# Zeros moved behind a softmax, a band matrix copied in four pieces, and a new order of instructions

## The chip, the cores and the metric

The kernel runs on one core of one Trainium2 chip. The metric is the device time of one execution in microseconds (us). Before the change three runs gave 176.5, 177.24 and 177.67; the median is 177.24. A profile of one further execution was taken, which itself took 177.53.

Engines are named as the profile names them: PE multiplies matrices (PEld is its loading of the stationary operand), DVE and ACT work on vectors, POOL and SP issue DMAs here.

## The reference

Two stages follow each other on x (8 batches, 4224 tokens, 192 channels, float32). The first is a causal convolution over 7 tokens, with one set of 7 weights for each of 8 heads (24 channels each), the weights being a softmax. The second mixes tokens through a 64 wide product, without a softmax:

```python
w = np.exp(weight - weight.max(-1, keepdims=True)); w = w / (w.sum(-1, keepdims=True) + 1e-9)   # (8, 7)
y = np.einsum('hk,bskhg->bshg', w, x_unf).reshape(B, S, D)      # x_unf: the 7 tokens up to s, zeros ahead of the first
W_tok = (1 / np.sqrt(64)) * np.einsum('bsd,btd->bst', y @ w_q, y @ w_k)
out = np.maximum(np.einsum('bst,btd->bsd', W_tok, y), 0) @ w_out
```

Since nothing non-linear stands between W_tok and y, the token by token matrix is never formed: W_tok y is (y w_q) (w_k^T y^T y), and y^T y is a 192 x 192 Gram matrix.

## The kernel before

**Tiling.** Tokens of a batch are cut into 35 chunks of 122 (NCC, CW); a chunk is loaded as 128 rows, 6 of them from the chunk ahead, and cast to bf16 on its way into XW. Groups of chunks share a load: four groups of 9 (the last of 8) in the first batch, two of 18 and 17 in the others. POOL issues all loads of x; SP issues the small weights and the stores.

**Steps of one batch**, with the kind that each has in the code and PE's matmuls in it:

- conv: for two heads, BAND (128 x 128 for each head, a banded matrix of the 7 softmax weights) times the group's columns, four matmuls; ACT or DVE copies the result from PSUM into Y (line 671).
- tr_lo, tr_hi: transposes of Y, channels 0 to 127 (16 matmuls for 8 chunks) and 128 to 191 (10 or 11), copied by DVE into YTL (698) and YTH (733).
- wq: y w_q from the transposes (lines 751 and 755), copied into WQT (771).
- gram: six chunks of Y times themselves, 18 matmuls (787), added up in a PSUM bank of their own.
- g, turn, gt, m, ms: the Gram matrix is copied, turned and multiplied with w_k, which gives the mixing weights MSB and MBD of the batch.
- mix_lo, mix_hi: WQT with the mixing weights (878, 890); ACT or DVE applies the relu on its way to RT (907, 908).
- fin_hi, fin_lo: RT times w_out (935 and the helper at 391, 392); the result is copied into one of four output buffers (970), and SP stores it (978).

PE works in one of two tilings of its array, 128x64 for most steps and 64x128 for mix_lo and fin_hi (COL2 and ROW2 in the code). Lines 391, 392 and 395, 396 are helpers that issue two half wide matmuls or transposes; conv, fin_lo, tr_lo and m all pass through them.

**What sets the order.** Each step is an Op with its engine, an assumed length, what it needs, and a due time vt, which is overwritten by the next number of the list TURNS. The Planner lays the Ops out engine by engine: among the Ops that can start it takes the one with the smallest vt, where a step of PE in the other tiling counts STAY more. Each engine then runs its own list in that order, with semaphores for what an Op needs from another engine; what is listed as `after` orders the plan without a wait of its own. Nothing is decided at run time. `op.lands` tells the Planner when a load of x is assumed to have arrived.

**The beginning.** DVE sets zeros and ones in many small buffers (lines 409 to 422), POOL makes an identity, DVE and PE make helper matrices from it. When the 56 convolution weights have landed, DVE computes their softmax (461 to 492) with ACT's exponential, and `taps` (494) spreads it. From it PE fills two PSUM banks, with eight matmuls each, that hold the bands; ACT copies one half and DVE the other into BAND (527). The first conv needs both.

Of the kernel before, what the change touches and what calls it, by code (L numbers as in the profile page):

```python
# [10 lines left out]


TURNS = [
    int(t) / 1000
    for t in """
-9360 -9860 -8870 -8880 -9260 -9760 -9760 -9160 -9060 -8960 -8910 -8910 -8860 -9360 -9310 -9360 -9360
-9300 -9290 -9280 -8360 -8260 -8210 -8360 -8160 -7960 -7910 -7860 -7360 -7260 -6960 -7260 -4360 -10360
-4260 -4160 -4060 -4040 -3360 -3260 -3160 -4360 -4360 -4360 -4360 -4360 -4360 -4360 -4360 -4360 -4360
-3360 -3340 -3260 -3240 -2360 -2340 -2260 -2240 -1360 -1340 -1260 -1240 -360 -340 -260 -240 640 660 740
760 1640 1660 1740 1760 2640 2660 2740 2760 -480 -5256 -3269 -5639 -2436 -6119 -4785 -6922 -2697 -6547  # L20
-2900 -8184 -3709 -11773 -2741 -3270 -6090 -11945 -3405 -6849 535 -5290 -3070 -5355 -2914 -5199 -4248
-3270 -5203 -8176 -5200 -3617 1049 7270 -1527 1452 -125 437 -1115 2575 669 4462 -4008 2241 -736 2188
-3392 2688 -366 4671 2314 4774 1510 -5859 -1080 1650 3655 -2805 -2225 2863 3712 -4982 -214 3624 -440
5811 168 -43 -4182 2328 1099 2977 4333 5544 2125 -4960 -5487 -5264 -3044 -1246 -5292 -632 -6217 -764
-74 -1078 1645 -1059 -604 310 -1847 1633 809 1261 1148 1774 613 1995 -221 2133 3240 -1868 3227 -220 725
-412 3895 1345 -3908 -437 2412 1145 -3912 1759 7529 -2401 -2511 -376 -45 -770 179 75 1157 1606 377 1178
2478 1419 2696 -2691 660 4785 4565 7183 -1945 323 1366 4118 -874 -955 202 -527 -342 -901 930 -907 356
2535 1985 1382 772 4127 1260 -1111 124 1160 1068 -949 2843 737 1947 1165 1141 1963 1865 1015 1391 1447
1702 -74 1049 2157 -573 -696 2171 3091 -3875 1621 1815 2057 1336 1560 3406 350 3930 1811 1631 806 1533
-2176 120 -160 307 697 392 -607 2158 1443 1095 4683 784 2578 2771 4703 2742 7357 3260 5899 3463 6217  # L30
3645 8560 -333 6048 2165 -3227 -299 4804 1442 -269 2464 1033 2330 -2282 2380 4417 716 -49 3007 5023
2635 1331 4441 4948 2995 6849 3538 5333 2785 2768 -3179 -2909 4430 6167 8185 2441 2170 3478 2909 2541
554 -2341 2444 1927 -821 1930 2471 1683 3865 3015 2812 1681 1913 2901 2236 -1040 2160 2775 2437 2022
2264 1982 2456 530 2945 -625 83 2391 2437 -247 4869 10274 3843 686 -2295 3278 468 -2877 2621 3234 3552
5619 5142 2314 3447 -712 2811 2566 3158 2537 2842 2785 -1373 2551 2194 3151 4852 2972 5013 3067 6779
3044 1235 3763 8267 3776 5123 4769 7025 4778 6514 4876 4862 2843 3189 4464 -186 3400 3287 1517 170 3082
4632 173 2822 4141 2345 4919 -1156 3870 4328 3579 2730 2456 3119 1411 4084 5177 4842 -327 4148 4784
2483 12403 11388 12726 1688 187 6372 10131 3246 4258 -1702 3458 4182 -118 2930 2729 1882 4669 8253 3861
3544 1615 3872 -172 2986 3160 3716 -1740 4531 9062 4005 3598 4951 3990 4363 2435 3391 -188 774 5121
6256 1049 3585 3961 4077 3890 4171 3621 2923 4666 7097 2748 2343 3820 2734 3811 2033 5780 3818 8021  # L40
2648 2954 4015 5571 3280 -1286 3326 1296 4205 -77 4486 1455 4875 3311 5075 4171 5445 4695 5467 3840
5547 6065 4545 4764 3889 874 4988 5384 3296 1407 5065 3706 4229 1167 4799 5495 -1008 2735 5015 4824
-216 1086 4797 3220 6247 4075 6903 8096 2585 2446 2397 3366 12419 11466 9645 4504 4002 2353 3004 4592
2447 1923 4855 3304 3544 3930 4268 4563 -31 1642 3776 4290 -862 3100 4826 6478 4160 4860 2445 3040 6705
3413 4148 6792 4180 4104 2785 4391 4686 4414 786 5937 2381 5714 4010 4678 4791 3602 4621 5486 -3702
4694 4691 4776 4745 8565 4811 2733 1579 4439 3726 3846 1552 3006 3416 5091 3731 3114 391 4950 -191 4947
1241 5561 6938 5922 7844 6076 5816 6857 5549 6431 8495 5919 4361 1180 965 5336 3713 5074 2853 2377 5685
3499 1703 6336 5580 6743 3976 5914 890 3735 -850 6119 5447 4947 4119 5702 6592 2952 2914 3851 5062
11027 10134 10283 4336 4832 2354 5585 5204 5235 5902 4279 5332 6811 4930 5452 70 7184 7777 5311 5310
3592 2752 3699 4914 5160 5093 886 6992 7265 5826 4610 2412 5386 6402 2677 5391 5863 3510 6078 4797 3048  # L50
3549 7308 4286 5112 2810 5621 5940 3872 3652 3847 6176 6516 2312 5811 4551 3444 5310 2800 3910 6703
2902 3118 6150 4601 5838 5604 6069 7926 5802 5058 6795 5408 6694 6497 7055 7466 7544 6117 8040 8562
2857 4878 6430 1709 6339 6247 4084 2149 3587 4651 7375 5911 5923 8233 4224 5104 7135 8548 7626 1422
6752 7520 5954 8811 9981 10001 3331 2861 1100 5523 5736 7942 8989 6855 6991 3418 3771 5267 6754 6792
5257 8583 2774 5930 5621 6098 8589 5981 7588 10163 5667 7262 8790 2009 6160 6573 7890 9275 9286 4367
8366 1994 4430 8376 2928 6391 6798 7671 9079 8471 6945 8447 929 3104 8245 1738 6621 7113 7765 8298
10610 7609 8976 2499 6811 5339 3124 4383 3701 4861 7650 5674 5118 6955 3022 7026 1967 7057 1554 7391
6867 7378 5794 8478 7540 10493 11198 10567 7886 9868 8667 7608 6132 7813 12143 8053 10500 4734 5726
10278 10809 6108 7660 6892 9279 8811 10480 9400 11789 6610 6051 11636 12987 12320 10573 10429 10064
11172 6766 7180 6653 8881 8940 8302 8163 3734 5115 8337 5917 10881 1732 6196 10991 548 6570 3947 6628  # L60
5684 11786 5374 8456 5972 5205 7358 2365 6800 7531 8553 12143 9541 7507 4239 2615 6653 8229 3661 7031
8556 8852 7269 9218 4711 5758 2449 5650 7927 7690 7261 10545 9140 8476 10487 4525 3241 2208 7451 8457
7788 6544 11624 6678 6638 3216 7890 3616 6282 3822 7930 5698 8782 6900 4062 5129 6641 6131 8120 8832
8094 4423 8160 8786 8210 8027 5877 5536 6062 1738 8351 8563 8713 4799 8391 5602 10941 9278 9705 9844
6685 7724 8581 9175 4769 3738 8621 7276 9572 10940 8347 11120 8993 5619 8811
""".split()
]

# [35 lines left out]
class Planner:  # L104
# [3 lines left out]
    LAT = {"PE": 240.0, "ACT": 145.0, "DVE": 140.0, "POOL": 150.0, "SP": 0.0}  # L108
    SWITCH = 145.0

    STAY = 0.865

    HOLD = 1

    def __init__(self, nbank, first_bank):
        self.ops = []
# [163 lines left out]
def bass_lightweight_conv__then__hypermixer_token_mlp_kernel(  # L280
# [9 lines left out]
    H, KC = weight.shape  # L290
# [15 lines left out]
    t = 0  # L306
# [37 lines left out]
    BAND = sbuf("band", [128, H, 128], BF16)  # L344
# [29 lines left out]
    def bank(i, n=1):  # L374
        return PS[:, i * 512 : (i + n) * 512]

    def add(*a, dma=None, kind=None, **k):
        op = Op(*a, **k)
        op.dma = dma
        op.kind = kind  # L380
        op.vt = TURNS[len(planner.ops)]
        return planner.add(op)
# [11 lines left out]
    def turn_halves(e, out, in_, identity):  # L394
# [11 lines left out]
        vt=-9,  # L406
# [3 lines left out]
    zero_w = add("DVE", lambda e, op: e.memset(WQT[64:128, :, wq_cols[-2] :], 0.0), 150, vt=-8.51)  # L410
# [15 lines left out]
        lambda e, op: e.affine_select(  # L426
            IDENT[:, :], IDENT[:, :], [[-1, 128]], ALU.is_equal, 0.0, base=0, channel_multiplier=1
        ),
        1250,
        needs=[one],  # L430
        vt=-9,
    )
# [22 lines left out]
    own = add(  # L455
        "DVE",
        lambda e, op: e.tensor_reduce(OWN[:, :], IDENT[:, :].rearrange("p (k i) -> p i k", i=16), AX.X, ALU.add),
        200, needs=[ident], vt=-8.92)


    mx = add("DVE", lambda e, op: e.tensor_reduce(WMX[:, :], WT_F[:, :, :], AX.X, ALU.max), 150, needs=[load_w], vt=-8)
# [39 lines left out]
    )  # L501
    taps.needs.append(own)


    bands = []
    for q0, engine in ((0, "ACT"), (4, "DVE")):

        def spread(e, op, q0=q0):
            last = None
            for q in range(q0, q0 + 4):  # L510
                last = halves(
                    e,
                    bank(op.bank)[:, (q - q0) * 128 : (q - q0 + 1) * 128],
                    STEPT[0:112, 112 - 16 * q : 240 - 16 * q],
                    TAPS[0:112, :, :].rearrange("p i h -> p (i h)"),
                    start=q == q0,
                    stop=q == q0 + 3,
                    skip_group_check=True,
                )
            return last  # L520

        fill = add("PE", spread, 260, needs=[taps, stept], banks=1, vt=-7 + 0.1 * q0)

        def band(e, op, q0=q0, fill=fill):
            dst = BAND[:, :, 16 * q0 : 16 * q0 + 64]
            src = bank(fill.bank).rearrange("p (j h) -> p h j", h=H)
            return e.copy(dst, src) if op.engine == "ACT" else e.tensor_copy(dst, src)  # L527

        bands.append(add(engine, band, 550, drains=fill, vt=-6.9))


    load = {}
    at = [5000.0]

    def gen_load(b, gi):
        sem = semaphore(f"s_x{b}_{gi}")
# [19 lines left out]
                )  # L556
            )

        at[0] += len(cs) * 260.0
        load[b, gi] = []  # L560
        for k, part in enumerate(parts):
            first = (b, gi) == (0, 0) and part[0].shape[1] > 1 and len(part[0].shape) == 3
# [7 lines left out]
                vt=-10 if first else -4 + b + gi * 0.1 + 0.02 * k,  # L570
            )
            op.tail = 1500.0
            op.lands = at[0]
            load[b, gi].append(op)

    for gi in range(len(groups_of(0))):
# [482 lines left out]
```

## Time and profile before

| | us |
|---|---|
| median of three runs (lowest, highest) | 177.24 (176.5, 177.67) |
| the profiled execution | 177.53 |
| its span, first to last instruction | 175.7 |
| first convolution on PE | 8.76 |
| first record of the granted clock at full speed | 15.10 |
| last load of x landed | 106.0 |
| last matmul ended | 170.84 |
| last store landed | 175.13 |

The span is 1.8 us shorter than the execution's own time, since it counts from the first instruction to the last. All times in views are from the beginning of the span. A line of the timeline gives start, length, engine, line of the kernel, operation, what it writes and reads, and how often in a row; idle time of the engine before it and what ended that stand in brackets. [...]

In the list of loads, x of the first batch lands at 6.77, 10.79, 13.13 and 15.14 in its four groups, and of the second at 21.30 and 25.59.

### The profile page before, as it was taken

Reading aid. Unit: us, or ns where it says so; the run is one execution under the profiler, and the core shown is the slowest. Engines: PE = TensorE matmul, PEld = TensorE weight load, DVE = VectorE, ACT = ScalarE, POOL = GpSimd, SP = SyncE. Lnnn points to the kernel's source line nnn. Section 1 sums busy time; section 2 is a strip of 40 time slices with the busy share of each in tenths; the row PEclk is TensorE's granted clock in tenths of the full one; section 3 lists DMA queues with packets and bytes.
Section 4 is the critical chain, followed back from the end, with each engine's and each line's share of the span. In section 5 each row is a group of like instructions: output and inputs, shape, how many; then the busy total and the mean of one; then the engine's idle time right before and its main releaser. Section 6 shows DMA issues by size and latency. Waiting matters only on the chain.

```text
span 175.7 us, 7099 instructions
## 1 busy us (share of the span) xinstructions
PE 157.1 (89%) x3226; PEld 121.7 (69%) x3226; DVE 118.0 (67%) x216; ACT 123.5 (70%) x206; POOL 30.3 (17%) x39
## 2 busy tenths in 40 slices
PE   0289799888999999899989979999999999999990
PEld 0179666776787787668778766878767777877550
DVE  6556587765766677586787738689688675765740
ACT  3243677597787948668648747888888896698980
POOL 7999452524230000000000000000000000000000
PEclk9999999999999999999999999999999999999995
DMA  3999999999999999999999999067283045987787
GB/s 30 162 189 186 205 191 193 191 196 277 193 279 194 286 309 268 343 250 243 304 264 282 237 194 348 24 244 297 103 343 127 4 175 216 356 347 309 265 303 262
DMA packets 48157, 40.36 MB, mean 230 GB/s; under 512 B 37632, under 2 KB 40960, under 8 KB 48128
## 3 DMA queue, kind: packets, MB, share of 16 engines
q0 software_dynamic: 36128, 13.61, 65.1%
q1 hardware_dynamic: 12000, 26.31, 40.9%
q8 instruction: 25, 0.41, 0.9%
q14 instruction: 4, 0.03, 0.1%
HBM read 27.56 MB, written 25.95 MB: 305 GB/s over the span
## 4 chain that ended last, share of the span: by engine, by line
PE 88%; issue 4%; DVE 3%; ACT 2%
PE ps L391 25%; PE ps L787 14%; PE ps L935 8%; PE ps L392 7%; PE ps L395 6%; PE ps L726 6%; PE ps L878 5%; PE ps L751 4%; PE ps L890 4%; PE ps L755 4%; PE ps L396 3%; ACT rt L907 1%; ACT out_sb L970 1%; DVE band L527 0%; DVE xw L416 0%
## 5 line engine op out<-in xcount | busy, mean ns | idle before, releaser
L970 ACT COPY out_sb<-ps 128x768 f32<-128x768 f32 (+1 forms) x46 | 34.7, 768 | 15.1 <-PE ps L392 11.3
L671 ACT CAST y<-ps 122x816 bf16<-122x816 f32 (+3 forms) x46 | 35.7, 791 | 13.2 <-PE ps L392 12.8
L907 ACT ACTIVATE rt<-ps 128x1024 bf16<-128x1024 f32 (+3 forms) x44 | 34.1, 800 | 6.4 <-PE ps L878 4.5
L787 PE MATMUL ps<-y 122*64 122x192 bf16 (+4 forms) x840 | 33.8, 222 | 2.2 <-issue 2.2
L970 DVE COPY out_sb<-ps 128x768 f32<-128x768 f32 (+1 forms) x26 | 21.6, 840 | 19.7 <-PE ps L392 18.5
L392 PE MATMUL ps<-wol,rt 128*64 128x192 bf16 x264 | 33.9, 255 | 1.0 <-issue 1.0
L787 PEld LDWEIGHTS ps<-y 122*64 122x64 bf16 (+1 forms) x840 | 31.1, 112 | 4.9 <-issue 2.8
L565 POOL DMA_DIRECT2D xw<-in_x_dram x34 | 29.9, 893 | 22.3 <-issue 21.5
L391 PE MATMUL ps<-wol,rt 128*64 128x192 bf16 x264 | 33.7, 255 | 0.0
L391 PE MATMUL ps<-xw,band 128*64 128x432 bf16 (+3 forms) x144 | 31.8, 335 | 1.5 <-DVE band L527 0.9
L392 PE MATMUL ps<-xw,band 128*64 128x432 bf16 (+3 forms) x144 | 32.1, 337 | 1.1 <-issue 1.1
L391 PEld LDWEIGHTS ps<-wol,rt 128*64 128x64 bf16 x264 | 24.1, 138 | 8.1 <-issue 2.0
L908 DVE TENSOR_SCALAR rt<-ps 128x512 bf16<-128x512 f32 (+3 forms) x36 | 23.6, 674 | 8.2 <-PE ps L878 7.6
L671 DVE CAST y<-ps 122x864 bf16<-122x864 f32 (+3 forms) x26 | 23.6, 912 | 8.0 <-PE ps L392 7.5
L698 DVE COPY ytl<-ps 128x976 bf16<-128x976 bf16 (+1 forms) x40 | 23.0, 591 | 3.9 <-PE ps L396 3.3
L392 PEld LDWEIGHTS ps<-wol,rt 128*64 128x64 bf16 x264 | 24.1, 138 | 1.2 <-issue 1.2
L396 PE MATMUL ps<-ident,y 122*64 122x122 bf16 x280 | 21.1, 219 | 0.0
L395 PE MATMUL ps<-ident,y 122*64 122x122 bf16 x280 | 21.0, 219 | 0.0
L935 PE MATMUL ps<-woh,rt 64*128 64x192 bf16 x264 | 20.4, 250 | 0.2 <-ACT rt L907 0.2
L395 PEld LDWEIGHTS ps<-ident,y 122*64 122x64 bf16 x280 | 18.1, 112 | 2.0 <-issue 0.5
L726 PE MATMUL ps<-ident,y 122*64 122x122 bf16 (+1 forms) x344 | 17.1, 220 | 1.3 <-DVE y L671 0.7
L396 PEld LDWEIGHTS ps<-ident,y 122*64 122x64 bf16 x280 | 17.7, 112 | 0.0
(95 smaller groups left out, 218.8 us busy)
## 6 DMA issues: line engine op xcount, KB each, us to landing
out_dram<-out_sb SPq DMA_DIRECT2D x28, 768.0 KB, 5.1
xw<-in_x_dram POOLq DMA_DIRECT2D x7, 816.0 KB, 33.2
xw<-in_x_dram POOLq DMA_DIRECT2D x7, 768.0 KB, 33.7
out_dram<-out_sb SPq DMA_DIRECT2D x8, 384.0 KB, 3.3
xw<-in_x_dram POOLq DMA_DIRECT2D x2, 432.0 KB, 8.3
out_dram<-out_sb SPq DMA_DIRECT2D x8, 96.0 KB, 4.3
xw<-in_x_dram POOLq DMA_DIRECT2D x1, 384.0 KB, 5.2
xw<-in_x_dram POOLq DMA_DIRECT2D x8, 45.8 KB, 25.0
```

The lines of the kernel that those rows point to most:

```text
L391: e.matmul(out[0:64], lhsT[:, 0:64], rhs, **k)
L392: return e.matmul(out[64:128], lhsT[:, 64:128], rhs, **k)
L395: e.transpose(out[0:64], in_[:, 0:64], identity)
L396: return e.transpose(out[64:128], in_[:, 64:128], identity)
L565: lambda e, op, part=part: e.dma_start(*part),
L671: return e.copy(dst, src) if op.engine == "ACT" else e.tensor_copy(dst, src)
L726: last = e.transpose(ps[64 * i : 64 * i + HI, o : o + w], Y[0:w, yb, c, LO:D], IDENT[0:w, 0:w])
L787: mm = e.matmul(bank(GB)[p : p + 64, o : o + z - r], Y[0:w, yb, c, r : r + 64], Y[0:w, yb, c, r:z], start=st, stop=end, skip_group_check=True,
L907: return e.activation(dst, src(), AF.Relu)
L908: return e.tensor_scalar(dst, src(), 0.0, None, op0=ALU.max)
L935: last = e.matmul(bank(op.bank + a)[:, o : o + D], RT[64 * a : 64 * a + HI, slot, 2, i:n:nt], WOH[64 * a : 64 * a + HI, :], start=i == q, ...
L970: return e.copy(dst, src) if op.engine == "ACT" else e.tensor_copy(dst, src)
```

## The change

Four things change; the functions for the steps of a batch do not.

1. The zeros for WQT, WQH, YTH, WKT, WKB and MBD (six small memsets on DVE) are put behind `taps` with an `after`. They come ahead of the copies of the bands on DVE. `own` gets a later due time and stays ahead of the softmax in DVE's list.
2. The bands are filled in four PSUM banks with four matmuls each, and copied in four pieces of 256 columns, by ACT, DVE, ACT and DVE.
3. The times at which the Planner takes loads of x to have landed are other constants, for the first batch a list, for the others one every 5.5 us, where it was 0.26 us for each chunk.
4. STAY is 1.057229 instead of 0.865, and all of TURNS for the steps of the batches is new, so that the order of all engines is another one. The work of PE is the same, matmul for matmul, but the two tilings follow each other in 94 places instead of 106. Which of ACT and DVE does a copy changes in some places.

In the new order PE begins, after the four conv steps of the first nine chunks, with the Gram step of chunks 0 to 5, a tr_hi and the tr_lo of chunks 0 to 7, then the four conv steps of the second nine chunks, then the Gram step of chunks 6 to 11. Before, after the first four conv steps there came a tr_hi, the second four conv steps, the Gram step of chunks 0 to 5, tr_lo, tr_hi and tr_lo.

```diff
-    STAY = 0.865
-
-    HOLD = 1
+    STAY = 1.057229
+
+    HOLD = 1.000000
...
+    for zero in (zero_w, zero_q, zero_yt, *zero_k, zero_m):
+        zero.after.append(taps)
...
     bands = []
-    for q0, engine in ((0, "ACT"), (4, "DVE")):
+    for q0, engine in ((0, "ACT"), (2, "DVE"), (4, "ACT"), (6, "DVE")):

         def spread(e, op, q0=q0):
             last = None
-            for q in range(q0, q0 + 4):
+            for q in range(q0, q0 + 2):
                 last = halves(
...
-                    stop=q == q0 + 3,
+                    stop=q == q0 + 1,
...
-        fill = add("PE", spread, 260, needs=[taps, stept], banks=1, vt=-7 + 0.1 * q0)
+        fill = add("PE", spread, 200, needs=[taps, stept], banks=1, vt=-7 + 0.1 * q0)

         def band(e, op, q0=q0, fill=fill):
-            dst = BAND[:, :, 16 * q0 : 16 * q0 + 64]
-            src = bank(fill.bank).rearrange("p (j h) -> p h j", h=H)
+            dst = BAND[:, :, 16 * q0 : 16 * q0 + 32]
+            src = bank(fill.bank)[:, 0 : 32 * H].rearrange("p (j h) -> p h j", h=H)
...
-        bands.append(add(engine, band, 550, drains=fill, vt=-6.9))
+        bands.append(add(engine, band, 340, drains=fill, vt=-6.9))
...
-    at = [5000.0]
+    LANDS = [6000.0, 9900.0, 12300.0, 13900.0]
...
-        at[0] += len(cs) * 260.0
...
-            op.lands = at[0]
+            op.lands = LANDS[gi] if b == 0 else 13900.0 + 5500.0 * (2 * b + gi - 1)
```

The lists TURNS are left out: 50 lines of numbers before, 81 after, read as thousandths before and as millionths after.

## The prediction

> **What bounds the kernel now.** I read the page first: busy times, DMA queues, the chain that ended last.
>
> ```profile
> PE 157.1 (89%) x3226; PEld 121.7 (69%) x3226; DVE 118.0 (67%) x216; ACT 123.5 (70%) x206; POOL 30.3 (17%) x39
> ...
> q8 instruction: 25, 0.41, 0.9%
> ...
> PE 88%; issue 4%; DVE 3%; ACT 2%
> ```
>
> PE is the chain. ACT and DVE have 30% to spare; "issue" is time on PE that no wait explains. Keep the second line in mind: 25 packets, 0.41 MB, are instructions on their way to an engine. Then the waits of PE:
>
> ```profile
> PE ps L787 <- issue: 2.2, 2, 1.3
> PE ps L392 <- issue: 2.1, 2, 1.1
> PE ps L391 <- DVE band L527: 0.9, 1, 0.9
> PE ps L726 <- DVE y L671: 0.7, 1, 0.7
> ```
>
> From its first convolution at 8.76 us to its end at 170.84 PE waits visibly for another engine only three times (0.70, 0.20, and the 0.9 ahead of the first). The other gaps are "issue", six of 0.5 to 1.3 us. They fall inside a run of matmuls that wait for nothing, as here inside one Gram step:
>
> ```profile
> 20.48 0.54 PE L787 MATMUL ps<-y 122*64 122x192 bf16 x12 [1.28 <-issue]
> ```
>
> Numbering the matmuls of the trace, the six gaps stand before numbers 221, 474, 601, 1237, 1619 and 1874: apart by 2, 1, 5, 3 and 2 times about 127 matmuls. With one weight load each and a few waits that is 256 instructions, and 16,384 bytes (each packet of q8 in the trace) over 256 is 64. So PE's program comes in **blocks** of 256 instructions, and these gaps end when a block comes in: the q8 packets start at 18.01, 30.78, 37.69, 68.66, 87.76 and 100.72, the gaps end at 20.48, 33.15, 40.15, 70.96, 90.19 and 103.09, each 2.3 to 2.5 later (starts from the trace's DMA records). While x loads, a packet starts 3.3 to 4.4 us after PE entered the block before it. A block therefore can't follow its forerunner in under some 3.8 + 2.4 = **6.2 us** (5.7 to 6.8). After the last x load (106.0) the first part falls to 2.6 or less, and no such gap is left.
>
> ```profile
> 15.10:103.09 87.99, 82.58 (x1781) 65.17 (x1777) 61.58 (x105) 61.94 (x108) 16.39 (x19) 1.00 1.42 246
> 103.09:170.84 67.75, 67.55 (x1352) 50.34 (x1352) 47.90 (x81) 56.70 (x90) 0.00 (x0) 1.00 0.61 226
> ```
>
> Columns: the stretch, its us, then PE, PEld, DVE, ACT and POOL busy (count), clock, DMA share, GB/s. The DMA share falls from 1.42 to 0.61 at 103; PE loses 5.4 us before and 0.2 after.
>
> [...]
>
> **The change, part by part.** Beginning of the trace, DVE:
>
> ```profile
> 3.02 0.11 DVE L417 MEMSET wqh<- 128x64 uint32 x1
> ...
> 3.42 0.12 DVE L435 COPY step<-ident 128x128 bf16<-128x128 bf16 x1
> ...
> 4.28 0.11 DVE L411 MEMSET yth<- 64x64 uint32 x1
> ...
> 4.70 0.15 DVE L461 TENSOR_REDUCE wmx<-wt_f 128x8 f32<-128x56 f32 x1
> ...
> 7.93 0.69 DVE L527 CAST band<-ps 128x512 bf16<-128x512 f32 x1 [1.16 <-PE ps L392]
> ```
>
> *Zeros.* Three stand in 3.02 to 3.42 and three in 4.28 to 4.70: 0.40 + 0.42 = 0.82. Without them the reduce starts at 3.88; the taps it needs landed at 3.75 and the mask is through (POOL, 2.70). taps then ends at 5.94 instead of 6.76. The zeros follow it, 0.82, until 6.84. Their readers (weight casts, products, masks of the mix) come after 15 us: no cost there. POOL's loads wait only for the zeros of xw, which stay, and SP's weight loads for x (10.79): neither queue moves.
>
> *Bands.* Spreads: 16 matmuls in 1.07, so the four pieces are ready at about 6.4, 6.65, 6.85 and 7.1. A copy of 256 columns isn't in the trace; it lies between half of the 512-column ones (0.29 ACT, 0.35 DVE) and the whole (0.58, 0.69). On the slope from the 432-column y copies (0.52, 0.62) I take 0.38 and 0.45. ACT: 6.45 to 6.85, then to 7.25. DVE is held by the zeros until 6.84, then 7.3 and 7.75 to 7.8. First convolution at 7.95 (+0.14, as 8.62 to 8.76) against 8.76: **0.8 earlier** (0.6 to 1.0). Its x landed at 6.77.
>
> *Order at the start.* Before, the four convolutions of the first 9 chunks are followed by a wait for their copies, a transpose, then the next four convolutions, and a Gram step and a transpose cover the second set of copies. Now the Gram step (0.96), both transposes (0.51, 0.81) come first, then the four convolutions (1.44), then a Gram step that needs them at once: a second wait. 7.95 + 2.35 (8.76 to 11.11) = 10.30, + 2.28 = 12.58, last convolution issued 13.66, its copy ready at + 0.61, DVE 0.62, Gram step at **14.95**. Before, PE was equally far on, bar one transpose, at 14.8 to 14.95. So the head start is spent on the new wait. It goes deeper: matmul 94, the first of that Gram step, begins a block in both orders (14.74 before). The block after it was held by its fetch until 20.48. Asked for at 14.95 it comes at 14.95 + 6.2 = 21.1; asked for already with the last convolution (13.93), at 20.1. The trace doesn't say which; I take the middle, **+0.1** (-0.4 to +0.6).
>
> *The new order after that.* PE's work is unchanged but for changes between its two tilings, 106 before, 94 now. Rows: a Gram step lasts 0.515 ahead of one of its own tiling and 0.63 ahead of the other; fin_lo 0.383 and 0.483; fin_hi 0.192 and 0.270. Some 0.08 to 0.14 each, and 5 of the 12 fall before 103 us, 7 after. I laid the median lasting of each kind of step along both orders and cut them into blocks. From 14.74 to 103.09 there are 14: work 80.3, but with no block under 6.2 the sum is 88.3; measured 88.35. The new order: work 79.7, with the floor 88.0, so **-0.3** where work alone would give -0.6. After 103: 67.2 against 66.7, **-0.6**. The cover here is ACT and DVE staying ahead; the distances between a copy and its next reader are as tight in both orders (31 and 39 with less work between than their own rows last, by under 0.2 mostly). x lands 2 us or more before each convolution needs it. The last store follows PE by 4.8 as before (one 0.80 copy, 3.4 to land): 0.
>
> Sum: +0.1 - 0.3 - 0.6 = **-0.8**. The profiled execution took 177.53 (span 175.7 and 1.8 around it): 176.7. The median of the runs is 177.24; from it 176.4, which I give.
>
> **The rivals.** *Fetches come sooner* (0.2 less, 6.0): the same block sum gives 86.0, so 80.0 without the first block against 82.1, and the second block starts 0.6 earlier than before: -0.6 - 2.1 - 0.6 = -3.3, 173.9. For it: single fetches took 5.7. Against: x loads are issued as before, and they fill the DMA queues.
>
> *Fetches come later*: stores of the new order fall where they delay packets in the load stage. At 6.4 the sum is 90.4, 84.0 without the first: +1.9, start +0.8, end -0.6: +2.1, **179.3**. It decides from 6.28 on, where the 0.8 is used up. For it: 6.8 was seen once, and stores move. Against: the three runs of before lie within 1.2, which leaves the mean only 0.1 of play.
>
> *The clock.* Convolution pairs take 0.36 until 15.10, where the first record of the granted clock stands, and 0.185 after. PE had worked without a gap from 11.11. The second wait breaks this: counted from 14.95 the same 4.0 us end at 18.9, and the fetch still hides it (work of the block 4.1, so 19.04 + half of 3.95 = 21.0). Past 18.9 it costs half of what is added: counted as the 6.34 from the first convolution it is 21.3, block at 22.2, +1.7 - 0.9 = +0.8, 178.0.
> [...]
>
> **How the numbers follow.** Forecast 0.54 (176.4, own range 175.4 to 177.5); sooner fetches 0.15; later fetches 0.18; clock 0.13. 1% is 1.8 us (about what this measurement tells from no change): under 175.5 lie the sooner fetches and a tail of the forecast's, 0.22; over 179.0 most of the later fetches, 0.14; within, 0.64. The range 174.2 to 178.8 cuts the far halves of both fetch cases.
>
> **What would show it.** Right: first convolution near 7.95; a wait of 0.6 to 0.7 before the second Gram step at 14.95; the first gap of the second block ending near 20.6; six or more "issue" gaps, all before 106, at steps of 127 matmuls; 14 blocks in 88. Wrong: few such gaps, or blocks following faster than 5.7 in the load stage; waits for ACT or DVE over 1 us in all after 20 us; clock past 19.

## The result: 4.5% slower

The changed kernel takes 184.89 us (median of four runs, 184.28 to 185.44), the kernel before 176.9 in four runs beside it (176.5 to 177.67). The ratio is 1.0446, with a 95% interval of 1.0392 to 1.0499. Forecast were 176.4 and a range up to 178.8: the sign was wrong, and the time lies far above the range.

The span of the profiled execution is 183.4 us, where it was 175.7: 7.7 more. The lines of its page that answer to those shown of before:

```profile
PE 160.2 (87%) x3226; PEld 123.4 (67%) x3226; DVE 118.5 (65%) x216; ACT 124.1 (68%) x208; POOL 30.3 (17%) x39
...
PEclk9999999999999997899999999999999999999996
...
q8 instruction: 25, 0.41, 0.9%
...
PE 69%; DMA 11%; ACT 7%; DVE 6%; issue 3%; ACTq 0%; DVEq 0%
```

The work and the instruction packets are the same. Two things are new. The chain that ended last, which was 88% PE, now has 11% of DMA in it, and the granted clock falls for two slices in the middle (7 and 8 tenths). The waits, of PE and then of all engines, say which DMA:

```profile
PE ps L422 <- ACT out_sb L1004: 3.4, 1, 3.4
...
PE ps L785 <- DVE ytl L732: 2.6, 1, 2.6
```

```profile
ACT out_sb L1004 <- DMA out_dram<-out_sb: 6.0, 2, 4.9
...
DVE out_sb L1004 <- DMA out_dram<-out_sb: 4.1, 2, 2.7
```

Columns: who waits for whom, us in all, how many times, the longest. Line 1004 copies a finished tile of the output from PSUM into one of four output buffers. These copies waited for stores: until a store has read its buffer out, no copy may write it again. (Before, one such wait stood on ACT, 2.4 us, and PE didn't notice it.) How that reaches PE is in the chain, with start, length and what ran (a part):

```profile
59.42 0.80 ACT out_sb L1004
60.22 0.03 ACT gt L840
60.25 8.61 DMA out_dram<-out_sb
...
68.93 0.81 ACT out_sb L1004
69.74 0.14 issue
69.87 0.34 PE ps L422
...
75.52 0.81 ACT out_sb L1004
76.33 0.02 issue
76.35 7.68 DMA out_dram<-out_sb
...
84.12 0.36 DVE out_sb L1004
84.48 0.60 DVE rt L942
85.08 0.58 DVE ytl L732
85.66 0.04 issue
85.71 0.41 PE ps L785 x2
```

A store is issued at 60.25 and takes 8.61 us. Its buffer is the one that ACT's next copy writes (both name the same semaphore in the trace, one of the four that belong to the buffers), so that this copy begins at 68.93, 4.91 us after ACT's last work. It empties a PSUM bank, and the next convolution writes into that bank: PE stands still for 3.45 us until 69.87. At 76.35 it happens again: a store of 7.68 us holds a copy of DVE, which is only 192 columns wide; behind it in DVE's list stands the copy into YTL (732) that the products of line 785 need, and PE waits 2.57 us.

The two waits are not of one kind. The kernel gives a tile its buffer by the tile's number (`n_out % NOUT`), and the new order takes tiles out of their sequence. By the semaphores of the stores, two of the four buffers had been read out at 57.13 and 60.58, and were written again only at 69.63 and 80.51: while ACT stood until 68.93 for the buffer of its tile, two others were free. At 84.03, when the second store landed, the other three were held until 86.61, 89.24 and 92.32: there all four were taken.

The third price is the clock. A window of the changed kernel (columns as in the prediction's fence of windows):

```profile
70.98:74.39 3.41, 3.41 (x27) 2.19 (x23) 1.12 (x2) 1.83 (x3) 0.00 (x0) 0.50 1.59 194
```

From 1.1 us behind the end of the wait of 3.45 us PE works 3.41 us at half clock (0.50); a pair of the products of lines 785 and 789 begins every 0.43 us there (71.21 to 72.49) and every 0.22 at 1.00 (22.94 to 23.59). So it does the work of some 1.7 us, an estimate from these. 3.45 + 2.57 + 1.70 = 7.7, just what the span has grown by. It is not the whole account, though: small gains and losses around it cancel. Counted at the beginnings of PE's instruction blocks (start of the same matmul number in both traces, counted from 0; starts, since records of matmuls overlap: one begins at 69.87 and is 0.34 long, the next begins at 69.88):

| block begins at matmul | before | after | lost so far |
|---|---|---|---|
| 221 | 20.48 | 21.28 | 0.80 |
| 602 | 40.28 | 40.23 | -0.05 |
| 1111 | 64.85 | 65.13 | 0.28 |
| 1238 | 70.96 | 76.56 | 5.60 |
| 1493 | 83.79 | 92.35 | 8.56 |
| 1874 | 103.09 | 109.73 | 6.64 |
| PE's end | 170.84 | 177.51 | 6.67 |
| end of the span | 175.7 | 183.4 | 7.7 |

The same number is not the same work, since the steps come in another order. By the mean lengths of the steps (an estimate from the traces) the two orders have done the same work within 0.1 us at 221 and 1874, while at 602 and 1111 the new one has done 0.8 to 1.3 us less. So by the count it is within 0.3 of before at 40 and 65 us, and by the work some 1 us behind. Then by the count it loses 8.3 in 27 us, gets 1.9 back by 109.73 (while PE stands, the loads of x go on: x is all in at 97.9, before at 106.0), keeps the rest until PE ends, and loses 1.0 more between PE's end and the last store.

### The profile page after: what moved, and what is told of

It is laid out like the page before. It is cut to its first block, busy times and chain, and to the rows that moved or that the text cites. A ratio compares the mean times of both kernels' runs of the same rounds, so it can differ in the third digit from the quotient of the medians.

```text
span 183.4 us, 7094 instructions
## 1 busy us (share of the span) xinstructions
PE 160.2 (87%) x3226; PEld 123.4 (67%) x3226; DVE 118.5 (65%) x216; ACT 124.1 (68%) x208; POOL 30.3 (17%) x39
## 3 DMA queue, kind: packets, MB, share of 16 engines
q0 software_dynamic: 36128, 13.61, 62.4%
q1 hardware_dynamic: 12000, 26.31, 38.9%
## 4 chain that ended last, share of the span: by engine, by line
PE 69%; DMA 11%; ACT 7%; DVE 6%; issue 3%; ACTq 0%; DVEq 0%
PE ps L422 19%; PE ps L821 12%; DMA out_dram<-out_sb 11%; PE ps L969 6%; PE ps L423 5%; PE ps L426 5%; PE ps L785 5%; PE ps L760 4%; PE ps L912 4%; PE ps L789 4%; PE ps L924 3%; ACT out_sb L1004 2%; ACT y L705 2%; ACT rt L941 2%; PE ps L427 2%
## 5 line engine op out<-in xcount | busy, mean ns | idle before, releaser
L705 ACT CAST y<-ps 122x864 bf16<-122x864 f32 (+3 forms) x51 | 39.2, 793 | 16.3 <-PE ps L423 15.8
L1004 ACT COPY out_sb<-ps 128x768 f32<-128x768 f32 (+1 forms) x44 | 31.6, 735 | 17.8 <-PE ps L423 9.9
L1004 DVE COPY out_sb<-ps 128x768 f32<-128x768 f32 (+1 forms) x28 | 25.5, 914 | 18.6 <-PE ps L423 14.2
L422 PE MATMUL ps<-xw,band 128*64 128x432 bf16 (+3 forms) x144 | 33.1, 349 | 4.2 <-ACT out_sb L1004 3.4
L423 PE MATMUL ps<-xw,band 128*64 128x432 bf16 (+3 forms) x144 | 33.4, 351 | 0.0
L599 POOL DMA_DIRECT2D xw<-in_x_dram x34 | 29.9, 909 | 19.7 <-issue 18.9
L422 PE MATMUL ps<-wol,rt 128*64 128x192 bf16 x264 | 31.6, 253 | 0.0
L423 PE MATMUL ps<-wol,rt 128*64 128x192 bf16 x264 | 31.6, 253 | 0.0
L705 DVE CAST y<-ps 122x816 bf16<-122x816 f32 (+3 forms) x21 | 19.0, 905 | 9.0 <-PE ps L423 8.5
L426 PE MATMUL ps<-ident,y 122*64 122x122 bf16 x280 | 22.1, 221 | 0.8 <-issue 0.8
L427 PE MATMUL ps<-ident,y 122*64 122x122 bf16 x280 | 22.0, 222 | 0.0
L426 PEld LDWEIGHTS ps<-ident,y 122*64 122x64 bf16 x280 | 18.8, 113 | 3.0 <-issue 1.2
L422 PEld LDWEIGHTS ps<-xw,band 128*64 128x64 bf16 x144 | 15.1, 122 | 8.2 <-issue 4.1
L805 DVE CAST wqt<-ps 128x512 bf16<-128x512 f32 (+1 forms) x19 | 11.0, 581 | 12.3 <-PE ps L789 12.1
```

Of the source, the lines that this page charges most:

```text
L422: e.matmul(out[0:64], lhsT[:, 0:64], rhs, **k)
L423: return e.matmul(out[64:128], lhsT[:, 64:128], rhs, **k)
L426: e.transpose(out[0:64], in_[:, 0:64], identity)
L427: return e.transpose(out[64:128], in_[:, 64:128], identity)
L599: lambda e, op, part=part: e.dma_start(*part),
```

## The experiments

In all of them the order of every engine is a written list that is replayed, so that an edit doesn't make the Planner choose anew. In the diffs of that list a number is a step, the letter its engine (P, A, D, G, S for PE, ACT, DVE, POOL, SP), and behind it may stand the first PSUM bank. All ratios are to the kernel before on the same chip, with 95% intervals.

The theory: the new order fills output buffers in bursts, and while x loads a store holds a buffer for long (the six of 768 KB that the changed kernel issued from 58 to 82 us took 7.68 to 10.58), so that four buffers are too few for it. Its rivals: the delay comes from instruction fetches or from the clock, and the waits for buffers only stand where PE would have been late anyway; or the second wait at the start pushes the whole plan out of step.

### Six output buffers in the changed kernel

```diff
-    NOUT = 4
+    NOUT = 6
```

> The changed kernel, its order of instructions kept word for word, with six output buffers instead of four, so that a copy into an output buffer waits for the store six before it and not four. Theory A (output buffers): the two waits of PE that go back to a store (3.45 and 2.57 us) go, and with them the stretch at half clock behind the first (1.7): 184.9 - 7.7 = about 177, 175.5 to 178.5. Theory B (the new order itself, its waits at the start, its late clock, fetches of instructions): the buffers matter little, 183 to 185.

178.56 us, ratio 1.0057 (1.0031 to 1.0083): of 4.5% too much, 3.9 are gone. After 20 us, no wait of PE for line 1004 or 732 is left. The same two stretches, first in the changed kernel, then with six buffers:

```profile
69.00:75.00 6.00, 5.13 (x59) 3.61 (x61) 1.12 (x2) 4.19 (x6) 0.00 (x0) 0.72 1.60 193
82.00:87.00 5.00, 2.43 (x42) 1.48 (x38) 2.39 (x5) 2.08 (x3) 0.00 (x0) 1.00 1.15 343
```

```profile
69.00:75.00 6.00, 5.16 (x113) 3.93 (x109) 3.27 (x7) 4.45 (x6) 0.00 (x0) 1.00 1.57 208
82.00:87.00 5.00, 4.28 (x89) 2.92 (x85) 3.17 (x5) 3.01 (x7) 0.00 (x0) 1.00 1.28 282
```

In the same two windows PE gets through 113 matmuls instead of 59, and 89 instead of 42; the clock is 1.00. ACT's timeline with six buffers shows when that copy could have run:

```profile
64.90 1.58 ACT L1081 COPY out_sb<-ps 128x768 f32<-128x768 f32 x2 [1.24 <-PE ps L500]
```

Line 1081 is 1004 in the longer file. The pair that began at 68.93 now begins at 64.90, and what it waits for is PE. So the store alone held it, for some 4 us, and through it PE. The stores themselves are no faster (the one issued at 59.89 takes 8.47): a buffer was missing, not bandwidth. The burst shows as well: this run issues five stores within 6.8 us (70.68 to 77.51), where the kernel before never issued five within less than 10.9 us while x loaded. For the first wait a buffer for each tile in the order of use, with four as before, might have done as well, since two stood free; that was not run.

### Six, and three, in the kernel before

```diff
-    NOUT = 4
+    NOUT = 6
```

> The kernel before, its order kept, with six output buffers. Theory A: its only wait for a store (2.4 us on ACT) was covered, so nothing changes, 176.2 to 177.2 against 176.9. Rival: the kernel before loses to stores as well, under 175.5.

177.77 us, 0.9996 (0.9962 to 1.0029). The old order has no use for more: its 2.4 us of waiting on ACT was covered. So the 3.9% is the new order's own fault, and not a bound that both share.

```diff
-    NOUT = 4
+    NOUT = 3
```

> The kernel before, its order kept, with three output buffers. Theory A: a copy now waits for the store three before it, which takes 6 to 10 us to land while x loads; by the landing times of before four of the copies would wait 0.5 to 1.9 us, and PE behind them: 178.5 to 182. Rival (stores are not what an order has to fear): within 1 of 176.9.

183.36 us, 1.0339 (1.0269 to 1.0408), more than was expected. The old order with one buffer less becomes nearly as slow as the new one with four, and in the same way. Waits of PE, and the clock:

```profile
PE ps L966 <- ACT out_sb L1046: 3.4, 2, 3.2
...
PE ps L954 <- DVE out_sb L1046: 1.6, 1, 1.6
PE ps L1011 <- ACT out_sb L1046: 1.2, 1, 1.2
```

```profile
92.44:95.85 3.41, 3.41 (x32) 2.20 (x34) 1.72 (x4) 1.40 (x2) 0.00 (x0) 0.50 1.59 195
```

Again a wait for a copy into an output buffer (1046 is that line here), the longest 3.20 us until 90.71, and 3.41 us of half clock behind it. The half clock, 1.7 us, is a part of what came on top of the expectation. So four buffers in the old order is the last number that hides the stores, and little slack was left for another order to use.

### The new beginning alone

The changed kernel's code with the old order; only the zeros stand behind `taps`, and the bands are copied in four pieces.

```diff
-    for q0, engine in ((0, "ACT"), (4, "DVE")):
+    for q0, engine in ((0, "ACT"), (2, "DVE"), (4, "ACT"), (6, "DVE")):
...
+    for zero in (zero_w, zero_q, zero_yt, *zero_k, zero_m):
+        zero.after.append(taps)
```

> The order of before with the new beginning alone (zeros behind the softmax, bands in four pieces). Theory: PE starts 0.8 us earlier and, the order behind it being the old one, nothing eats this: 176.0 to 176.5. Rival (the zeros or the four pieces cost time later): 177.5 or more.

176.96 us, 0.9973 (0.9937 to 1.0009): too close to call. It was run again, in more rounds:

> The order of before with the new beginning once more, beside the last, with more rounds since its first interval, 0.9937 to 1.0009, still holds no change. Theory (head start of 0.8 us passed on): 0.995 to 0.997. Rival: 0.999 to 1.001.

176.68 us, 0.995 (0.9919 to 0.9981): a gain of 0.9 us, about the whole head start of the first convolution (7.91 instead of 8.76). PE ends at 170.10 instead of 170.84. With the old order behind it, the head start isn't lost: the first part of the change is worth what it saves.

### The start of the new order put back

The changed kernel with six buffers, where the second four convolutions come ahead of the first Gram step (145) and tr_lo (115, 116) again:

```diff
-84A 57G 88D 145P 58G 125P2 115P3 59G 126D 42S 95P4 97P5 116D 91P6 96A 93P0 60G 98D 92A 94A 61G 43S
+84A 57G 88D 58G 125P2 59G 126D 42S 95P4 97P5 91P6 96A 93P0 60G 98D 92A 94A 61G 43S 145P 115P3 116D
```

> The changed order with six output buffers, and at the start the second four convolutions put ahead of the first Gram step and of the transpose behind it, as before the change; everything else in its place. Theory (second wait at the start): without the wait of 0.67 ahead of the Gram step at 14.95 PE enters its second block near 14.0 and the clock rises a window earlier or so; all blocks come 0.7 to 0.9 earlier: 1.0057 of the run with six buffers goes to about 1.001. Rival (the fetch of the second block or the late clock don't depend on it): no change, 1.004 to 1.008.

177.47 us, 0.9982 (0.9951 to 1.0013), against 1.0057 without it: some 0.75%, 1.3 us, though the two were measured on two chips. The first record of the full clock stands at 13.86, where six buffers alone had 18.99, and the second block begins at 19.84 (21.0). PE ends at 170.14 (170.78).

These are single executions, and the time of the clock's rise varies: with few loads (below) the beginning with the second wait had it at 16.20. The forecast's +0.1 was net of a head start of 0.8, so that it put the second wait at 0.9; the ratios say 1.3, and the two ends of PE 0.64. And now both of the change's faults are repaired, but the new order is no faster than the old one with the new beginning: PE ends at 170.14 and 170.10.

### Idle matmuls ahead of the first convolution

Since the start seemed to hang on the clock, 20 matmuls whose results nobody reads were put into PE's idle time at the beginning, on the old order with the new beginning. They write the bank of the Gram matrix, which is free then.

```diff
+    def idle(count, cols):
+        def emit(e, op):
+            last = None
+            for _ in range(count):
+                last = e.matmul(bank(GB)[0:128, 0:cols], STEPT[:, 0:128], STEPT[:, 0:cols], start=True, stop=True)
+            return last
+
+        return emit
+
+    add("PE", idle(9, 240), 1500, needs=[zero_s], vt=-9.8)
+    add("PE", idle(11, 240), 1500, needs=[stept], vt=-7.9)
```

> The order of before with the new beginning, and 20 matmuls without use (128 x 240, into the free Gram bank) while PE waits ahead of its first convolution: nine from 1.3 us, eleven from 3.7 us. Clock theory: they count as work, the clock rises before 8.8 instead of near 15, and the first 94 matmuls take 1.4 us less: 0.988 to 0.992 of before. Rival 1: the clock doesn't count them, 0.997 as without them. Rival 2: the fetch of the second block sets its start and isn't earlier, 0.995 to 0.998. The block theory expects the gaps of PE without a releaser 20 matmuls earlier in the program, before number 221 counted with the 20, thus 201 of the old count.

174.56 us, 0.9843 (0.9791 to 0.9896): better than expected, and faster than both kernels. PE's timeline:

```profile
1.29 1.98 PE L1125 MATMUL ps<-stept 128*128 128x240 bf16 x9 [1.29 <-DVE stept L520]
...
3.88 2.07 PE L1125 MATMUL ps<-stept 128*128 128x240 bf16 x11 [0.28 <-ACT stept L553]
...
7.91 0.25 PE L499 MATMUL ps<-xw,band 128*64 128x216 bf16 x1 [1.07 <-DVE band L638]
```

```profile
16.48 0.24 PE L504 MATMUL ps<-ident,y 122*64 122x122 bf16 x1 [0.83 <-issue]
```

The first record of the full clock stands at 5.49. The first convolution starts at 7.91 as without the matmuls but its record is 0.25 us long instead of 0.36, and the second block of instructions begins at 16.48, where it was 19.70. The gap there is a test of the blocks, too: it stands before matmul 221 with the 20 new ones counted, which is number 201 of the old count. So in this run the gap went by the number of instructions and not by what they do.

### Six buffers for that version

```diff
-    NOUT = 4
+    NOUT = 6
```

> The order of before with the new beginning, the 20 matmuls without use, and six output buffers. With an earlier start the copies reach their buffers earlier, while the stores land when the loads of x let them; if that costs PE something, six buffers give 0.2 to 0.5 of a per cent: 0.979 to 0.983. Rival (covered as in the kernel before): as without, 0.984.

174.43 us, 0.9854 (0.9784 to 0.9923): no further gain. Faster at the start, the old order still lives with four. In this execution the clock rose at 6.67, fell to half from 10.08 to 13.50, and rose again, with the same order of instructions, behind two waits of only 0.86 and 0.85 us; the second block began at 16.96 instead of 16.48, and at matmul 602 both are at 35.80.

### The end, and everything together

The stores at the end: the smallest tile of the output was put last and its copy given to DVE, on the changed kernel with six buffers and the old start.

```diff
-986D 954S 971P0 965D 967P4 987P6 973A 988P 968P 966S 969D 989A 979P2 990S 980P 970S 975P0 981A 976P
-977A 982S 978S
+986D 954S 971P0 965D 967P4 973A 968P 966S 969D 979P2 980P 970S 975P0 981A 976P 977A 982S 978S 987P6
+988P 989D 990S
```

> The last kernel of the changed order (six buffers, restored start), and at the end the smallest output tile (128 rows, 98 KB) put last and copied by DVE, as in the order before; the rest in its place. Theory (the last store of 393 KB is issued 0.6 us behind another one and lands 4.5 us later, where before a small one landed after 3.4): from PE's last matmul to the end of the span 4.8 to 5.0 instead of 5.9, 0.992 to 0.995 of before. Rival (the stores at the end are crowded whichever is last): 5.6 to 5.9, 0.997 to 0.999.

177.53 us, 0.9981 (0.9955 to 1.0006): no gain. From PE's end to the end of the span it takes 5.54 instead of 5.88, and the kernel before 4.82.

Then that version with the 20 idle matmuls, so that all that the runs had shown to help stands on the new order:

```diff
+    add("PE", idle(9, 240), 1500, needs=[zero_s], vt=-9.8)
+    add("PE", idle(11, 240), 1500, needs=[stept], vt=-7.9)
```

> The changed order with six buffers, restored start, the small tile last, and the 20 matmuls without use. If the new order saves 0.9 us of PE's work by its 12 changes of tiling less, it ends 0.3 to 0.5 per cent under the order of before with the same beginning: 0.978 to 0.981. Rival (the floor of the fetches takes the saving): 0.983 to 0.986.

176.54 us, 0.9937 (0.9907 to 0.9968), slower than both the expectation and its rival, and 1.2% slower than the old order with the same help on the same chip (174.43). PE ends at 168.75 against 167.84, the last store comes 5.46 behind it against 4.55. A good part of PE's difference is one gap:

```profile
43.28 0.36 PE L500 MATMUL ps<-xw,band 128*64 128x408 bf16 x1 [1.57 <-issue]
```

It stands at a block's beginning, and the q8 packet for it starts at 40.70, 4.5 us after PE entered the block before (3.3 to 4.4 in the kernel before): one fetch that started later, in one execution. Whether the new order brings it every time was not looked into.

### Hardly any loads of x

To see what makes the stores and the fetches slow, both kernels were run with x loaded for three batches only; the convolutions of the other five take the x of these again, so that five outputs are those of other batches. All other work stays.

```diff
-            gen_load(b, gi)
+            if b < 3:
+                gen_load(b, gi)
+            else:
+                load[b, gi] = [x for g in range(len(groups_of(b % 3))) for x in load[b % 3, g]]
...
-                        XW[:, b, c0 : c0 + n, GRP * h : GRP * h + GRP],
+                        XW[:, b % 3, c0 : c0 + n, GRP * h : GRP * h + GRP],
```

The changed kernel, with its four buffers:

> The changed kernel, order and four buffers as they are, but x is loaded for the first three batches only; the other five convolve the x of these three again (their outputs are those of other batches). All other work, PE's, the copies and the stores, stays. Loads end near 39 us. Theory (stores are slow because loads of x hold the DMA queues, and four buffers then run out): stores after 40 us land in under 5 us instead of 7 to 10, both waits of PE (3.45 and 2.57) and the half clock behind the first go, and no gap for fetched instructions comes after 45 us: 184.9 - 7.7 - 3.9 (work of blocks 5 to 14 by rows against their measured 63.3 in the run with six buffers) = 173 to 175, 0.975 to 0.988 of before. Rival (stores take their time without loads too): waits stay, 180 or more.

173.53 us, 0.9772 (0.9742 to 0.9802). The kernel before:

> The same with the order of before, four buffers: x of three batches only. Theory (a floor of about 6.2 us for each block of 256 instructions while x loads): from 40 us on PE needs its own work only, 59.1 by rows for blocks 5 to 14 instead of 62.9 measured: 3.9 less, 0.976 to 0.982 of before. Rival (no such floor; the gaps are something else): 0.995 to 1.0.

172.28 us, 0.9702 (0.9675 to 0.9728). The issues of whole tiles from 40 to 103 us (KB each, and the median us until they land), in the changed kernel, in it with few loads, and in the kernel before with few loads:

```profile
out_dram<-out_sb SPq DMA_DIRECT2D x11, 768.0 KB, 8.2
```

```profile
out_dram<-out_sb SPq DMA_DIRECT2D x12, 768.0 KB, 5.1
```

```profile
out_dram<-out_sb SPq DMA_DIRECT2D x13, 768.0 KB, 4.0
```

Beside the loads such a store takes 8.2 us, without them 4.0 to 5.1. (The kernel before has 8.0 in this stretch, too, and 4.3 after 103 us.) With that, the changed kernel has no wait of PE for an output buffer; its 3.45 and 2.57 are gone with four buffers. So it takes three things together: four buffers tied to tiles by number, loads that nearly double the time of a store, and an order that takes the tiles out of sequence and in a burst.

The same two runs test the blocks. The kernel before, and it with few loads, in one window, and then that one's whole stretch of ten blocks:

```profile
40.15:103.09 62.94, 60.47 (x1274) 47.16 (x1273) 44.13 (x73) 44.75 (x74) 4.56 (x6) 1.00 1.36 266
```

```profile
40.15:103.09 62.94, 62.94 (x1369) 49.86 (x1364) 47.41 (x81) 47.72 (x78) 0.00 (x0) 1.00 0.42 163
38.90:98.07 59.17, 59.17 (x1276) 46.91 (x1275) 44.42 (x75) 45.19 (x75) 0.00 (x0) 1.00 0.40 154
```

PE is busy without a break, and no "issue" gap is left after 33.12 us. The ten blocks from matmul 602 to 1874 take 59.17 instead of 62.81. The expectation's sum by rows alone, without a floor, was 59.1. Matmul by matmul, the two traces differ at six beginnings of blocks, by 0.15 to 1.23 us each and 3.6 in all, and the rest cancels; so it is not a general slowing by the loads. So what the prediction estimated as a floor of some 6.2 us for a block showed only while x loaded, and in this stretch it cost 3.6 us, as the prediction's blocks had it.

The new order takes 59.45 between the same two numbers, but by the mean lengths of the steps these hold some 0.8 us more work in it (8 more matmuls of convolutions, for one). From 221 to 1874, where the work agrees within 0.1, the two runs with few loads take 77.16 (21.04 to 98.20) in the new order and 77.61 (20.46 to 98.07) in the old one: there the new order is 0.45 faster.

## Why the prediction was wrong, point by point

**The step that failed: "The cover here is ACT and DVE staying ahead; the distances between a copy and its next reader are as tight in both orders".** It priced the reader of a copy and not what the copy itself waits for. A copy into an output buffer waits for a store (8.61 and 7.68 us long here), and ACT and DVE take their lists in order, so they don't stay ahead but stand. Measured: 3.45 + 2.57 us on PE. The rows of the kernel before were there, one in the list of DMA issues from 15.1 to 103.09 us and one in the waits:

```profile
out_dram<-out_sb SPq DMA_DIRECT2D x12, 768.0 KB, 7.7
```

```profile
ACT out_sb L970 <- DMA out_dram<-out_sb: 2.4, 1, 2.4
```

Stores of 7.7 us, and one wait of ACT for such a store: the sign of buffers with little slack. It was passed over because PE didn't wait for it. Six buffers, three buffers and few loads show it from three sides. Without that step the forecast would have been much nearer: with six buffers matmul 1874 begins at 103.17, where before it was 103.09, +0.08 for a forecast of +0.1 - 0.3 = -0.2, and the ratio is 1.0057.

**"Waits for ACT or DVE over 1 us in all after 20 us"** was named as what would make the forecast wrong, and it did; but no rival went that way. The rival that was slower, "fetches come later", had the right place (the load stage, stores of the new order), 179.3 as its time and the wrong mechanism.

**The clock.** A fall in the middle was not foreseen. It adds 1.7 us to a wait of 3.45. Behind that wait and behind one of 3.20 (three buffers) the granted clock was 0.50 for 3.41 us. A wait of 2.57 (changed kernel) and a gap of 1.83 before 20.48 (three buffers) brought no fall, but near the start of the run with idle matmuls and six buffers two waits of 0.86 and 0.85 were followed by 3.41 us at 0.50, too. So the length of a pause alone doesn't decide it, and what does was not shown. In the traces of both kernels the changes of the clock lie whole multiples of 3.41 us apart: 157.01 us before (46 times 3.413, from 15.10 to 172.11), and 51.20, 3.41 and 105.81 in the changed kernel (15, 1 and 31 times, from 19.78 by 70.98 and 74.39 to 180.20). At the start the clock rose at 19.78, past the 18.9 up to which it was to cost nothing: 4.83 us after the Gram step at 14.95, where the prediction had counted 4.0 or 6.34, and with few loads, in the same order, 1.26 after it (16.20, 14.94), so that neither count held. The prediction's rule of "half of what is added" gives +0.4 for it, so a block at 21.4, and it began at 21.28 with PE busy all the way.

**"+0.1" for the start.** The first convolution came at 7.91 (7.95 forecast) and the Gram step, with its wait of 0.67, at 14.95 (14.95). PE's timeline:

```profile
7.91 0.36 PE L422 MATMUL ps<-xw,band 128*64 128x216 bf16 x1 [0.64 <-DVE band L561]
...
14.95 1.17 PE L821 MATMUL ps<-y 122*64 122x192 bf16 x18 [0.67 <-ACT y L705]
```

The block behind it began at 21.28, 0.8 later than before instead of 0.1. Most of that is the fetch and not the clock: in the changed kernel with few loads the clock rose at 16.20 already, and the block still began at 21.04, behind a gap of 1.24 that no other engine ended, 6.1 us after the Gram step at 14.94. That is the first of the prediction's two cases, 14.95 + 6.2 = 21.1; the middle between the two was the wrong choice, and the late clock adds 0.24. The start put back was worth 1.3 us by the two ratios (on two chips) and 0.64 at PE's end, where the forecast had 0.9 with the head start in it; which of these holds is not settled.

**"-0.3" for the load stage and "-0.6" behind it.** With buffers and start repaired, the blocks from 221 to 1874, which hold the same work within 0.1, take 82.67 in the new order (19.84 to 102.51), and 82.63 in the old one with the new beginning (19.70 to 102.33): nothing of the -0.3. With few loads it is 77.16 against 77.61, -0.45 of the 0.6 by work alone: most of that saving is there, and does not show while x loads. From matmul 1874 to PE's end it is 67.63 against 67.77, and with few loads 67.70 against 67.73: -0.14 and -0.03 instead of -0.6. There the price of 0.08 to 0.14 for a change of tiling, read from steps ahead of their own and of the other tiling, doesn't add up over a whole order; what takes its place wasn't found. Each of these is one execution.

**"The last store follows PE by 4.8 as before: 0"**: it follows by 5.86, +1.0. The last six stores take 2.7 to 4.5 us, the very last 4.19; in the kernel before 3.3 to 3.5, the last 3.40. And the last is issued 1.23 behind PE's end instead of 0.89. Every version of the new order that was profiled has 5.46 to 5.88 there, with one exchange of tiles changing little. Why stores land later at the end of this order stays open.

**What was right**: the head start and its size (0.9 us by itself), the blocks (256 instructions by the prediction's count, gaps at steps of 127 matmuls; with 20 matmuls put ahead the gap came 20 earlier in the old count), and the estimated floor under a block while x loads: it cost 3.6 us in 63 beside the loads, and with few loads no gap was left after 33.12 us. These terms moved the forecast by 1 us or less, though; the one that cost 7.7 us stood outside the sum.

## What to carry to other kernels

When the order of instructions changes, count what each buffer is held for, the DMA that empties it included: for every buffer in a ring, the time from the issue of its store to the next copy into it has to exceed the time that the store takes in that stage, here 7.4 to 9.2 us in the median and up to 10.6 beside loads, and 4.0 to 5.1 in the median without. If buffers are given out by a tile's number, an order that takes tiles out of sequence can wait for one while others stand free. A wait of a side engine for a DMA that cost nothing was here the place where the next order broke, and both pauses of over 3 us on PE in the middle (3.45 and 3.20) were followed by 3.41 us at half clock, an estimated 1.7 us more each. Where PE is idle at the beginning, matmuls that nobody reads may pay: here 20 of them, in time that was free, gave 1.2% beyond the new beginning (174.56 against 176.68), and with it the lowest ratio of those versions that do the whole work (0.9843, 0.9791 to 0.9896).

## What the runs showed of the hardware

- Stores of 768 KB from 40 to 103 us took 7.4 to 8.2 us in the median while loads of x ran (8.0 before, 8.2 in the changed kernel and with six buffers, 7.4 with three in the old order; the longest of the changed kernel 10.58), and 4.0 and 5.1 in the two runs with few loads. By the page of the changed kernel the packets of the loads' queue took 62.4% of the span of 16 engines and those of the stores' queue 38.9%.
- After a pause of PE of 3.45 us (changed kernel) and one of 3.20 us (three buffers) the granted clock was 0.50 for 3.41 us, beginning 1.1 and 1.7 us after PE went on. After 2.57 us (changed kernel) it stayed at 1.00, but two pauses of 0.86 and 0.85 us near the start were followed by 3.41 us of 0.50, too (from 10.08 with six buffers and the idle matmuls, and not in the run with four).
- The first record of the full clock came at 5.49 to 6.67 us in three runs with matmuls from 1.29 on, and without these at 13.87 and 15.99 in two with the new beginning and the old order, at 13.93 to 16.11 in four with the old beginning, and at 16.20 to 19.78 in three with the second wait: up to 3.6 us apart in executions with the same beginning.
- From matmul 602 to 1874 PE took 62.81 us beside the loads and 59.17 with few loads. The two traces differ there at six beginnings of blocks, by 3.6 us in all, and with few loads no "issue" gap stands after 33.12 us.
